# Eight chunks rather than six by seven block products, with the second matrix's sums made in the last part

## The chip, the cores and the metric

The kernel runs on one core of a Trainium2 chip. Its time is the device time of one execution in microseconds. TensorE (PE in the profile) multiplies, VectorE (DVE), ScalarE (ACT) and GpSimd (POOL) do the elementwise work, SyncE (SP) issues the DMAs. "Before" is the kernel as it was, "after" the changed one.

## The reference, cut to what matters

Block-causal attention over 8 batches of 8 heads, 576 tokens, head size 64, and behind it one feed-forward pair of matrices with a leaky ReLU between them, over all 4608 tokens. Everything is fp32.

```python
def _attn_ref(q, k, v):                  # 8, 8, 576, 64
    scores = scale * np.matmul(q, k.transpose(0, 1, 3, 2))
    scores = np.where(block_i >= block_j, scores, -1000000000.0)   # blocks of 64
    scores = scores - np.max(scores, axis=-1, keepdims=True)
    attn = np.exp(scores)
    attn = attn / (np.sum(attn, axis=-1, keepdims=True) + 1e-09)
    return np.matmul(attn, v)

def _moe_ref(x, w_in, w_out):            # 4608 x 512, 512 x 2048, 2048 x 512
    h = x @ w_in
    g = np.maximum(0.01 * h, h)
    return g @ w_out
```

## The kernel before, in words

Every fp32 operand of the feed-forward part is held as two numbers of TensorE's fast format, a high and a low one (`wih`/`wil`, `woh`/`wol`, `xh`/`xl`, `gh`/`gl`), and a product is three matmuls: high by high, high by low, low by high. A pair is made by a cast (ScalarE or VectorE, L300 and L301) and a subtraction (VectorE or GpSimd, L314, L315, L947, L948).

The 4608 tokens are 18 chunks of 256. The first `NP` = 12 go the plain way, 8 units a chunk: `ffn1` (L898) makes two blocks of 128 of the 2048 hidden columns in 24 matmuls of 256 columns, the leaky ReLU (L913) and the split follow, and `ffn2` (L925) adds their part of the output into `p_o` in 12 matmuls of 512 columns. These units lie among the 64 heads of attention: `PACE` says how many heads go by per chunk, `LEAD` how many heads after its last token's head a chunk starts. Heads 0 to 13 use plain fp32 operands; from head 14 on (`PLAIN`) the scores are split products (L573), the probabilities are turned by VectorE and a trip through DRAM (L798, L815, L827), and L713 multiplies them with the values.

The last `2 * TAIL` = 6 chunks are done in pairs, in `tail`. A pair of chunks is a 2 x 2 block product, and Winograd's form makes it with seven block products rather than eight. `first8` makes the first matrix for unit `u` of pair `k` (L1110): seven products of six matmuls of 256 columns, whose results VectorE adds up (L1123) into buffers called `piles`, `more` and a half of `xin`; they are stored to DRAM (`gd`). `second8` (L1239) does the same for the second matrix, 8 steps a pair, four for each half `s`, and each half fills four PSUM banks over its four steps; in its last step `q` = 3 ScalarE copies product 0 out of its bank and VectorE adds the others (L1262). The banks are the list `spots`: half 0 of a pair uses the two banks of the tile `p_s` and the two of `p_v`, half 1 the single-bank tiles `p_h` and `p_o`. `first8` goes round all eight, five a unit. The framework puts in the waits, by what each instruction reads and writes of a tile.

The seven products need sums of blocks of the weights. `sums_ahead` makes them on VectorE while attention runs (L947, into the memory of `xr`), 16 sets, one for each of 8 units of each matrix, and stores them to DRAM (`td`, L986); `PRE0` and `PRE1` say from which head on and how often. In the last part `brought` loads them (L1032) and splits them: `combos` for the first matrix before the last part, `combos2` one block of the second matrix's during it, `combos3` the rest when the first matrix is through with their place. `inputs8` loads a pair's tokens into `x8`, `splits8` makes the seven left operands of them.

The order of the instructions on each engine is written out ahead of time by `Plan`: each step has a rank (for attention the head's number, for a unit the head number at which it is due, in the last part `TR` + 8 `k` + `u`), engines it may run on and an assumed duration, and a list scheduler takes the ready step of the lowest rank. The constants at the head of the file shift these ranks (`RL`, `RP`, `RN`, `RM`, `RG8`, ...). SP's DMAs go out in that order too, and one that waits holds up those behind it. `fourth_stage` gives the memory of attention to the last part.

Of the kernel before, what the change touches and what calls it, by code (L numbers as in the profile page):

```python
# [17 lines left out]
P = 128  # L18
# [6 lines left out]
CH = 256  # L25
# [35 lines left out]
LEAD = 10.984  # L61
LAG = 1.995
RS = -15.318
RG = -8.8
OFF1 = 3.579
SL1 = 23.854
AHEAD = 2.6
# [6 lines left out]
PADD = 4400.167  # L74
HOLD = 266.733
FILL = 235
FILLTO = -148.268
# [9 lines left out]
    [-0.34, -1.77, -1.04, -0.21, -0.2],  # L87
    [-0.63, -6.06, 3.68, 0.48, -3.29],
    [-0.36, -16.86, -0.22, -5.03, 3.79],
    [2.49, -2.84, 0.0, -0.15, -1.95],  # L90
    [1.23, -5.51, -1.24, -1.19, -0.63],
    [-0.02, -6.57, 0.81, -0.09, 1.74],
    [-0.83, 3.75, -0.44, 0.18, -1.57],
    [0.33, 11.3, 1.53, -0.3, 0.55],
    [0.15, 0.48, -1.15, 1.44, -3.96],
# [188 lines left out]
def attention_ffn(ctx: ExitStack, tc: tile.TileContext, q2: bass.AP, k2: bass.AP, qk: bass.AP, v: bass.AP, w_in: bass.AP, w_out: bass.AP, out: bass.AP):  # L284
# [667 lines left out]
    def sums_ahead():  # L952
# [7 lines left out]
        def ahead(j):  # L960
            u, y = j // 2, j % 2
            rank = PRE0 + PRE1 * j
            gate = [("head", min(int(rank), NH - 1))]
            k0, k1, k2, k3 = ([("spare", y, c)] for c in range(4))
            at = lambda c, n=1, y=y: xr.rearrange("p d s -> p (d s)")[:, (4 * y + c) * CH : (4 * y + c + n) * CH]
            if y == 0:
                w0, w1 = wkeys[("wi", u)], wkeys[("wi", u + NU)]
                side = lambda f, low: f32((wil if low else wih)[:, :, f * P : (f + 1) * P])
                four = lambda ap: ap.rearrange("p (d f) -> p d f", f=P)
                sum_of(WIDE, lambda: four(at(1, 2)), lambda: side(u, 0), lambda: side(u, 1), True, rank, w0 + gate, k1 + k2)  # L970
                for h, key in ((0, k0), (1, k3)):
                    part = lambda low, h=h: side(u + NU, low)[:, 2 * h : 2 * h + 2]
                    sum_of(CH, lambda h=h: four(at(3 * h)), lambda part=part: part(0), lambda part=part: part(1), True, rank, w1 + gate, key)
# [401 lines left out]
```

## Time and profile before

| | us |
|---|---|
| timed runs | 1055.57 (median), 1051.42, 1056.27 |
| profiled execution | 1052.72 |
| its span, first to last instruction | 1050.9 |
| PE busy | 1021.6 (97%) |
| PE weight loads busy | 906.6 (86%) |
| VectorE busy | 792.4 (75%) |
| ScalarE busy | 609.8 (58%) |
| GpSimd busy | 353.1 (34%) |

The profile is of one execution. Times are in us, single durations at times in ns. An engine's busy time is the union of its instructions; matmuls follow one another before the one ahead has left the array, so the rows' durations overlap, and the distance from start to start is what one costs. "Idle before" names what ended an engine's wait. The stretches used below: attention with plain fp32 heads until 158 us, with split heads until 732 us, the rest of the plain chunks until 793.5 us, the first matrix of the last part until 925 us, the second until the end.

### The profile page before, as it was taken

The numbers are of one execution on the slowest core, as the hardware profiler recorded it, in microseconds if no ns is written. First come the engines' busy times: TensorE is split into PE (matmuls) and PEld (weight loads), VectorE is DVE, ScalarE is ACT, GpSimd is POOL, SyncE is SP. The second block draws the span as 40 slices with busy tenths as digits, with TensorE's granted clock in tenths as the row PEclk, the third lists the DMA queues.
The fourth block names the chain that finished last, engine by engine and source line by source line (L and its number), as shares of the span: only waits on it lengthen the run. The fifth ranks groups of instructions, "written<-read, shape, count | busy, mean of one in ns | idle before, by whom it ended". The sixth has DMA issues, their size and how long they took to land.

```text
span 1050.9 us, 21285 instructions
## 1 busy us (share of the span) xinstructions
PE 1021.6 (97%) x7336; PEld 906.6 (86%) x7336; DVE 792.4 (75%) x2000; ACT 609.8 (58%) x1435; POOL 353.1 (34%) x347
## 2 busy tenths in 40 slices
PE   7979999999999999999999999999999999989998
PEld 5658889888988888888888888888898999989997
DVE  6888978688978888988898887787065546588774
ACT  7788868476656656666665567575263434443331
POOL 3344327244334434534244344252101223211000
PEclk9999999999999999999999999999999999999999
DMA  6564534766767677676667767674554456765451
GB/s 206 165 195 143 164 107 134 211 206 187 230 183 249 213 229 214 206 221 211 209 204 221 224 213 238 187 225 145 158 202 131 126 172 178 204 211 167 153 163 65
DMA packets 136859, 196.28 MB, mean 187 GB/s; under 512 B 15408, under 2 KB 107312, under 8 KB 136752
## 3 DMA queue, kind: packets, MB, share of 16 engines
q1 hardware_dynamic: 136752, 194.93, 60.7%
q8 instruction: 58, 0.95, 0.4%
q14 instruction: 49, 0.40, 0.1%
HBM read 112.92 MB, written 81.95 MB: 185 GB/s over the span
## 4 chain that ended last, share of the span: by engine, by line
PE 91%; DMA 4%; DVE 2%; ACT 2%; issue 0%; SPq 0%; DVEq 0%; ACTq 0%
PE p_h L898 26%; PE p_o L925 25%; PE p_v L713 7%; PE p_v L573 4%; PE p_s L573 3%; PE p_h L1239 3%; PE p_s L1239 3%; PE p_o L1239 2%; PE p_v L1110 2%; PE p_s L562 2%; PE p_s L1110 2%; PE p_v L1239 2%; PE p_h L1110 2%; PE p_o L1110 2%; PE p_v L668 2%; PE p_v L757 1%
## 5 line engine op out<-in xcount | busy, mean ns | idle before, releaser
L898 PE MATMUL p_h<-big,wih 128*128 128x256 f32 x1216 | 245.5, 280 | 0.4 <-ACT big L300 0.4
L925 PE MATMUL p_o<-woh,big 128*128 128x512 f32 x768 | 236.5, 394 | 0.0
L898 PEld LDWEIGHTS p_h<-big,wih 128*128 128x128 f32 x1216 | 199.0, 188 | 9.9 <-issue 2.2
L315 POOL TENSOR_TENSOR big<-piles,big 128x512 fp32r<-128x512 f32 x80 | 108.2, 1353 | 233.7 <-ACT big L300 216.9
L798 DVE STREAM_TRANSPOSE turn<-prow 128x128 f32<-128x128 f32 (+3 forms) x400 | 146.3, 398 | 16.7 <-POOL prow L633 6.3
L925 PEld LDWEIGHTS p_o<-woh,big 128*128 128x128 f32 x768 | 133.0, 188 | 21.7 <-issue 2.4
L898 PE MATMUL p_h<-big,wil 128*128 128x256 f32 x448 | 122.2, 278 | 0.0
L925 PE MATMUL p_o<-wol,big 128*128 128x512 f32 x384 | 119.5, 393 | 0.0
L913 ACT ACTIVATE piles<-p_h 128x512 f32<-128x512 f32 x96 | 57.2, 595 | 77.9 <-PE p_h L898 75.1
L603 ACT ACTIVATE prow<-p_s,nmrec 128x448 f32<-128x448 f32 (+4 forms) x150 | 83.0, 559 | 32.5 <-DVE nmrec L594 24.7
L633 POOL TENSOR_SCALAR prow<-prow,nmrec 128x448 f32<-128x448 f32 (+4 forms) x89 | 54.4, 618 | 121.2 <-DVE nmrec L620 103.1
L898 PE MATMUL p_h<-xh,wih 128*128 128x256 f32 x320 | 88.1, 280 | 0.0
L315 POOL TENSOR_TENSOR ks<-qk_in,ks 64x576 fp32r<-64x576 f32 x57 | 81.7, 1433 | 17.9 <-ACT ks L300 11.9
L898 PE MATMUL p_h<-xh,wil 128*128 128x256 f32 x320 | 87.4, 278 | 0.0
L603 ACT ACTIVATE prow<-p_v,nmrec 128x576 f32<-128x576 f32 (+1 forms) x150 | 71.5, 484 | 26.2 <-DVE nmrec L594 22.6
L925 PEld LDWEIGHTS p_o<-wol,big 128*128 128x128 f32 x384 | 72.1, 188 | 15.8
L898 PEld LDWEIGHTS p_h<-big,wil 128*128 128x128 f32 x448 | 84.3, 188 | 0.1
L713 PE MATMUL p_v<-turn,vt 128*64 128x256 f32 (+3 forms) x700 | 76.0, 368 | 0.0
L594 DVE TENSOR_REDUCE nmrec<-p_s 128x1 f32<-128x448 f32 (+4 forms) x150 | 72.1, 515 | 0.7
L713 PEld LDWEIGHTS p_v<-turn,vt 128*64 128x64 f32 x700 | 45.4, 137 | 27.9 <-issue 16.9
L635 ACT ACTIVATE prow<-prow,nmrec 128x192 f32<-128x192 f32 (+4 forms) x112 | 59.3, 550 | 11.3 <-DVE nmrec L620 10.8
L300 ACT CAST ks<-qk_in 64x576 fp32r<-64x576 f32 x63 | 42.3, 672 | 40.5 <-PE p_v L573 28.8
(269 smaller groups left out, 2293.7 us busy)
## 6 DMA issues: line engine op xcount, KB each, us to landing
way<-turn SPq DMA_DIRECT2D x50, 448.0 KB, 3.9
way<-turn SPq DMA_DIRECT2D x100, 168.0 KB, 3.7
turn<-way SPq DMA_DIRECT2D x100, 168.0 KB, 3.3
qk_in<-in_qk SPq DMA_DIRECT2D x50, 288.0 KB, 3.5
turn<-way SPq DMA_DIRECT2D x100, 112.0 KB, 3.4
out<-piles SPq DMA_DIRECT2D x36, 256.0 KB, 2.5
raw<-in_w_in SPq DMA_DIRECT2D x16, 512.0 KB, 4.0
raw<-in_w_out SPq DMA_DIRECT2D x16, 512.0 KB, 3.7
```

Of the source, the lines that this page charges most:

```text
L315: ("POOL", pool2(n), lambda: nc.gpsimd.tensor_sub(dst(), one(), two())),
L573: nc.tensor.matmul(ap, later["qs"][z][:, cols], moving, start=first, stop=last)
L594: [("DVE", dve(kw[t]), lambda t=t, ap=ap, flat=flat: nc.vector.tensor_reduce(nm[z][: qn[t], at_col[t] : at_col[t] + 1], ap[: qn[t]], axis= ...
L603: nc.scalar.activation(o, ap[: qn[t]], AF.Exp, bias=nm[z][: qn[t], at_col[t] : at_col[t] + 1], scale=1.0, accum_out=sums[z][: qn[t], at_co ...
L635: ("ACT", act(kw[t], True) + 108, lambda: nc.scalar.mul(p(), p(), by)),
L713: nc.tensor.matmul(dst, later["vt"][z][:, j], src, start=start, stop=stop)
L798: nc.vector.transpose(dst, src.rearrange("p (s b i) -> p s b i", b=4, i=32))
L898: nc.tensor.matmul(p_h[z][:, i, :], w[:, d, f * P : (f + 1) * P], (xl if x else xh[y])[:, d, :], start=first and k == 0 and (u > 0 or i == ...
L913: add([("ACT", act(512), lambda: nc.scalar.activation(g, p_h[z], AF.Prelu, alpha=0.01))], rank, [("h", z)], ["g"])
L925: nc.tensor.matmul(p_o[m], a[:, i, m * P : (m + 1) * P], w[:, u + NU * i, :], start=u == 0 and k == 0, stop=u == NU - 1 and k == 5,)
L1110: nc.tensor.matmul(bank()[:, :CH], stationary(j, u, w, d), operand(j, x)[:, d], start=j not in (4, 6) and n == 0, stop=n == 5, skip_group_ ...
L1239: nc.tensor.matmul(to(), operand(j, low)[0][:, x * P : (x + 1) * P], moving(j, us[x], w), start=q == 0 and m == 0 and j in opens, stop=q = ...
```

## The change

`TAIL` goes from 3 to 4: ten chunks go the plain way, and eight, in four pairs, by seven block products. The second matrix's block sums are no longer among the sets made under attention: `ahead` makes 8 sets, not 16, of the first matrix alone, and `combos2` makes those of the second in the first-matrix phase of the last part, at the units that `SUMS` lists (two in each pair), in the memory of `x8`, on VectorE or GpSimd as the scheduler picks (`op2`); it splits one block at once and stores the other three to DRAM, from which `combos3` loads them as before. In the last part four PSUM tiles of one bank each (`p_x`) take the place of `p_s` and `p_v`, which are given back in `fourth_stage`. The constants of the order have new values, and so have eight numbers of the table `FIRST` (shifts of the first ten heads), which are not shown. The first matrix's sums in `ahead` are the same lines with less indentation.

```diff
-RL = -2.305
-RP = 2.849
-RB = -0.783
-RT = 1.737
+RL = -2.097
+RP = 1.15
+RB = -4.837
+RT = 0.934
 RV = 1.064
-RX = -0.49
-RN = 1.414
-RF = 4.292
-PACE = [5.0, 5.0, 5.67, 4.14, 5.46, 5.0, 4.52, 5.0, 5.55, 5.39, 5.0, 5.17, 5.0, 5.0, 5.0, 5.0, 6.28, 4.59]
+RX = -1.789
+RN = -12.631
+RF = 4.76
+PACE = [6.0, 6.82, 6.0, 6.18, 6.0, 5.97, 5.97, 6.0]
 TWO = True
-TAIL = 3
+TAIL = 4
 TURNS = 4
 TR = 1000.0
-RG8 = -1.0
-RS8 = -3.0
-SUM0 = 2
-RC8 = -8.0
-PRE0 = 22.0
-PRE1 = 2.136
+RG8 = -0.854
+RS8 = -1.748
+SUMS = [1, 2, 9, 10, 17, 18, 25, 26]
+RC8 = -9.359
+PRE0 = 25.352
+PRE1 = 3.071
 PREBY = "DVE"
-RL8 = -6.0
-RT8 = -0.956
-RM = 11.181
-
-LEAD = 10.984
-LAG = 1.995
-RS = -15.318
-RG = -8.8
-OFF1 = 3.579
-SL1 = 23.854
-AHEAD = 2.6
+RL8 = -5.167
+RT8 = -1.106
+RM = -38.787
+
+LEAD = 10.295
+LAG = 2.586
+RS = -15.233
+RG = -9.514
+OFF1 = 2.228
+SL1 = 23.787
+AHEAD = 2.346
...
-PADD = 4400.167
+PADD = 3332.902
...
-FILLTO = -148.268
+FILLTO = -146.792
...
-    p_s = fixed([P, 2, 512], F32, "p_s", pool=psum)
-    p_v = fixed([P, 2, 512], F32, "p_v", pool=psum)
+    p_o = fixed([P, DM], F32, "p_o", 2, pool=psum)
+    pairs = ExitStack()
+    pool = pairs.enter_context(tc.tile_pool(name="pairs", bufs=1, space=PSUM, side="right"))
+    p_s = fixed([P, 2, 512], F32, "p_s", pool=pool)
+    p_v = fixed([P, 2, 512], F32, "p_v", pool=pool)
     p_t = [p_v[:, x] for x in range(2)]
-    p_o = fixed([P, DM], F32, "p_o", 2, pool=psum)
     wide = ExitStack()
     p_w = fixed([P, 2, 512], F32, "p_w", pool=wide.enter_context(tc.tile_pool(name="wide", bufs=1, space=PSUM, reuse_waits="tile")))
     p_h = []
...
     def fourth_stage():
-        for stack in (late, early, tied):
+        for stack in (late, early, tied, pairs):
             stack.close()
+        pool = ctx.enter_context(tc.tile_pool(name="single", bufs=1, space=PSUM, side="right", reuse_waits="tile"))
+        later["single"] = fixed([P, 512], F32, "p_x", 4, pool)
         pool = ctx.enter_context(tc.tile_pool(name="tail", bufs=1, reuse_waits="tile"))
         later["new"] = fixed([P, 3, ND, CH], F32R, "new", None, pool)
         later["x8"] = fixed([P, ND, WIDE], F32, "x8", None, pool)
...
         def sum_of(*args):
             op2(*args, by=PREBY)
-        def ahead(j):
-            u, y = j // 2, j % 2
-            rank = PRE0 + PRE1 * j
+        def ahead(u):
+            rank, y = PRE0 + PRE1 * u, u % 2
             gate = [("head", min(int(rank), NH - 1))]
...
-            else:
-                for x, f in enumerate((u, u + NU)):
-                    w = wkeys[("wo", f)]
-                    sum_of(WIDE, lambda x=x: at(2 * x, 2), lambda f=f: f32(woh[:, f]), lambda f=f: f32(wol[:, f]), True, rank, w + gate, k2 + k3 if x else k0 + k1)
-                sum_of(CH, lambda: at(0), lambda: at(1), lambda: at(0), False, rank, k1, k0)
-                sum_of(CH, lambda: at(1), lambda: at(3), lambda: at(1), False, rank, k3, k1)
-                sum_of(CH, lambda: at(3), lambda: at(3), lambda: at(0), False, rank, k0, k3)
-                sum_of(CH, lambda: at(2), lambda: at(3), lambda: at(2), False, rank, k3, k2)
-            add([("SP", ISSUE, lambda: nc.sync.dma_start(td[u][:, y], at(0, 4)))], rank, k0 + k1 + k2 + k3, [("td", u, y)], lag="pre")
-
-        for j in range(2 * NU):
-            ahead(j)
...
+            add([("SP", ISSUE, lambda: nc.sync.dma_start(td[u][:, 0], at(0, 4)))], rank, k0 + k1 + k2 + k3, [("td", u, 0)], lag="pre")
+
+        for u in range(NU):
+            ahead(u)
     def tail():
         flat = lambda ap: ap.rearrange("p a b -> p (a b)")
-        spots = [(("s", y), lambda y=y: p_s[:, y]) for y in range(2)] + [(("t", y), lambda y=y: p_v[:, y]) for y in range(2)]
+        spots = [(("one", y), lambda y=y: later["single"][y]) for y in range(4)]
         spots += [(("h", y), lambda y=y: flat(p_h[y])) for y in range(2)] + [(("o", y), lambda y=y: p_o[y]) for y in range(2)]
         cells = range(0, CH, BLK)
         xins = [("xin", e) for e in cells]
...
+        old += [(key, y) for key in ("s", "t") for y in range(2)] + [("one", y) for y in range(4)]
...
         def combos2(u, rank):
-            w0 = wkeys[("wo", u)]
-            brought(u, 1, rank, 1, lambda: woh[:, u, CH:], lambda: wol[:, u, CH:], [x for x in w0 if not x[1]], [x for x in w0 if x[1]])
+            w0, w1 = wkeys[("wo", u)], wkeys[("wo", u + NU)]
+            base = 4 * (u % 2)
+            at = lambda y, n=1: flat8()[:, (base + y) * CH : (base + y + n) * CH]
+            d8 = 2 * (u % 2)
+            c0, c1, c2, c3 = (in8(d8 + d, d8 + d + 1, h * CH, (h + 1) * CH) for d in range(2) for h in range(2))
+            for y, (f, w) in enumerate(((u, w0), (u + NU, w1))):
+                op2(WIDE, lambda y=y: at(2 * y, 2), lambda f=f: f32(woh[:, f]), lambda f=f: f32(wol[:, f]), True, rank, w, (c2 + c3) if y else (c0 + c1))
+            op2(CH, lambda: at(0), lambda: at(1), lambda: at(0), False, rank, c1, c0)
+            op2(CH, lambda: at(1), lambda: at(3), lambda: at(1), False, rank, c3, c1)
+            op2(CH, lambda: at(3), lambda: at(3), lambda: at(0), False, rank, c0, c3)
+            op2(CH, lambda: at(2), lambda: at(3), lambda: at(2), False, rank, c3, c2)
+            split(
+                CH, lambda: woh[:, u, CH:], lambda: wol[:, u, CH:], lambda: at(0), rank, c0,
+                [x for x in w0 if not x[1]], [x for x in w0 if x[1]],
+            )
+            add([("SP", ISSUE, lambda: nc.sync.dma_start(td[u][:, 1, CH:], at(1, 3)))], rank, c1 + c2 + c3, [("td", u, 1)], lag="in3")
         def combos3(u, rank):
             brought(u, 1, rank, 0, lambda: sum8(u, 0), lambda: sum8(u, 1), [("S", u, 0)], [("S", u, 1)])
...
                 splits8(k, TR + 8 * k - 2)
             for u in range(NU):
                 first8(k, u, TR + 8 * k + u)
-                y = 8 * k + u - SUM0
-                if y >= 0 and y % 2 == 0 and y // 2 < NU:
-                    combos2(y // 2, TR + 8 * k + u)
+                for y in range(NU):
+                    if int(SUMS[y]) == 8 * k + u:
+                        combos2(y, TR + SUMS[y])
                 if k == TAIL - 1:
                     combos3(u, TR + 8 * TAIL + u // 2 + RT8)
         for n in range(8 * TAIL):
```

## Rows read from the trace of the kernel before

**Rows 1.** Stretches of the span: us, busy us (instructions) of PE, PEld, DVE, ACT, POOL, clock, DMA
```profile
0.00:158.00 158.00, 142.98 (x954) 111.78 (x955) 130.75 (x320) 119.99 (x300) 59.47 (x68) 1.00 0.53 163
158.00:732.00 574.00, 573.90 (x3945) 501.88 (x3944) 474.48 (x1323) 365.71 (x914) 239.56 (x232) 1.00 0.68 207
732.00:793.50 61.50, 61.50 (x414) 53.76 (x413) 25.62 (x47) 26.89 (x55) 8.92 (x8) 1.00 0.53 171
793.50:925.00 131.50, 127.18 (x1064) 125.10 (x1062) 73.09 (x159) 56.06 (x122) 31.39 (x33) 1.00 0.59 171
925.00:1050.90 125.90, 116.09 (x969) 114.06 (x967) 88.42 (x153) 41.19 (x48) 13.80 (x8) 1.00 0.47 147
```

**Rows 2.** Two windows of 25 us, same columns: one under attention, one of the last part
```profile
425.00:450.00 25.00, 25.00 (x169) 21.57 (x168) 22.71 (x64) 16.46 (x43) 11.12 (x12) 1.00 0.69 202
...
950.00:975.00 25.00, 25.00 (x215) 25.00 (x214) 19.23 (x32) 9.25 (x11) 3.45 (x3) 1.00 0.57 175
```

**Rows 3.** Chain of waits in order of time, plain chunks: start us, us, what
```profile
149.11 2.83 PE p_h L898 x24
...
745.22 2.75 PE p_h L898 x24
747.97 4.12 PE p_o L925 x18
```

**Rows 4.** The same chain in the last part, second matrix
```profile
939.09 2.72 PE p_s L1239 x24
...
1000.58 2.83 PE p_h L1239 x24
1003.40 2.12 PE p_o L1239 x18
```

**Rows 5.** Waits of PE after 793 us: waiting, waited for, us in total, times, longest
```profile
PE p_v L1110 <- ACT more L300: 2.0, 1, 2.0
PE p_v L1239 <- DVE piles L1262: 1.5, 3, 0.5
...
PE p_o L1110 <- ACT more L300: 1.0, 1, 1.0
...
PE p_s L1239 <- ACT piles L300: 0.9, 2, 0.5
...
PE p_v L1110 <- DVE piles L1123: 0.4, 2, 0.2
```

**Rows 6.** Timeline near 981 us: start us, us, engine, line, operation, tiles [idle before]
```profile
980.53 0.87 PE L1239 MATMUL p_s<-sum,big 128*128 128x256 f32 x6
...
981.43 0.37 ACT L300 COPY piles<-p_s 128x256 f32<-128x256 f32 x1 [1.47 <-PE p_s L1239]
...
981.86 0.39 PE L1239 MATMUL p_s<-woh,big 128*128 128x256 f32 x1 [0.46 <-ACT piles L300]
```

**Rows 7.** Groups of VectorE, 158 to 732 us: count | busy us, mean ns | idle before
```profile
L947 DVE TENSOR_TENSOR xr<-xr 128x256 f32<-128x256 f32 x64 | 28.5, 445 | 0.2
L634 DVE TENSOR_SCALAR prow<-prow,nmrec 128x192 f32<-128x192 f32 (+4 forms) x66 | 27.5, 445 | 0.6
...
L321 DVE TENSOR_REDUCE p_v<-p_v 64x64 f32<-64x128 f32 x49 | 14.2, 289 | 25.8 <-PE p_v L573 25.5
L947 DVE TENSOR_TENSOR xr<-woh,wol 128x512 f32<-128x512 f32 x16 | 11.8, 748 | 0.0
```

**Rows 8.** Exponents and first block products (ns min/median/max, first to last start); a split's timeline
```profile
L603 ACT ACTIVATE prow<-p_v,nmrec x150: 293/411/756, 158.2 to 732.0; 128x576 f32<-128x576 f32 x50, 128x192 f32<-128x192 f32 x50, 64x64 f32<-64x64 f32 x50
...
764.78 0.62 ACT L300 CAST new<-x 128x512 fp32r<-128x512 f32 x1
...
L1110 PE MATMUL p_s<-new,wih x48: 276/281/281, 793.7 to 911.0; 128*128 128x256 f32 x48
```

**Rows 9.** Timeline near 787 us, VectorE and GpSimd
```profile
786.98 1.30 POOL L315 TENSOR_TENSOR big<-piles,big 128x512 fp32r<-128x512 f32 x1 [20.67 <-ACT big L300]
...
787.24 1.31 DVE L947 TENSOR_TENSOR wol<-wol,woh 128x256 fp32r<-128x256 f32 x1 [3.48 <-ACT woh L300]
```

More of the change, by code (lines that the diff above doesn't have):

```diff
@@ L86 @@
 FIRST = [
-    [-0.34, -1.77, -1.04, -0.21, -0.2],
+    [-1.37, -1.77, -1.04, -0.11, 7.51],
     [-0.63, -6.06, 3.68, 0.48, -3.29],
-    [-0.36, -16.86, -0.22, -5.03, 3.79],
+    [-1.46, -16.86, -0.22, -5.03, 3.79],
     [2.49, -2.84, 0.0, -0.15, -1.95],
-    [1.23, -5.51, -1.24, -1.19, -0.63],
+    [1.23, -5.51, -1.24, -1.19, 3.67],
     [-0.02, -6.57, 0.81, -0.09, 1.74],
     [-0.83, 3.75, -0.44, 0.18, -1.57],
-    [0.33, 11.3, 1.53, -0.3, 0.55],
-    [0.15, 0.48, -1.15, 1.44, -3.96],
+    [-1.45, 11.3, 1.44, -0.3, 0.55],
+    [0.15, 0.69, -1.34, 2.68, -3.96],
     [1.34, -0.81, -0.2, -0.65, -0.94],
@@ L958, in sum_of @@
             op2(*args, by=PREBY)
-        def ahead(j):
-            u, y = j // 2, j % 2
-            rank = PRE0 + PRE1 * j
+        def ahead(u):
+            rank, y = PRE0 + PRE1 * u, u % 2
             gate = [("head", min(int(rank), NH - 1))]
             k0, k1, k2, k3 = ([("spare", y, c)] for c in range(4))
[L965 to L973, printed above, removed]
-                sum_of(CH, lambda: at(3), lambda: at(0), lambda: at(3), True, rank, k0, k3)
-                sum_of(CH, lambda: at(0), lambda: at(1), lambda: at(0), False, rank, k1, k0)
-                sum_of(CH, lambda: at(1), lambda: at(3), lambda: at(1), False, rank, k3, k1)
-                sum_of(CH, lambda: at(2), lambda: at(2), lambda: at(1), False, rank, k1, k2)
-            else:
-                for x, f in enumerate((u, u + NU)):
-                    w = wkeys[("wo", f)]
-                    sum_of(WIDE, lambda x=x: at(2 * x, 2), lambda f=f: f32(woh[:, f]), lambda f=f: f32(wol[:, f]), True, rank, w + gate, k2 + k3 if x else k0 + k1)
-                sum_of(CH, lambda: at(0), lambda: at(1), lambda: at(0), False, rank, k1, k0)
-                sum_of(CH, lambda: at(1), lambda: at(3), lambda: at(1), False, rank, k3, k1)
-                sum_of(CH, lambda: at(3), lambda: at(3), lambda: at(0), False, rank, k0, k3)
-                sum_of(CH, lambda: at(2), lambda: at(3), lambda: at(2), False, rank, k3, k2)
-            add([("SP", ISSUE, lambda: nc.sync.dma_start(td[u][:, y], at(0, 4)))], rank, k0 + k1 + k2 + k3, [("td", u, y)], lag="pre")
@@ L988, in sums_ahead @@
-        for j in range(2 * NU):
-            ahead(j)
+            at = lambda c, n=1: xr.rearrange("p d s -> p (d s)")[:, (4 * y + c) * CH : (4 * y + c + n) * CH]
+            w0, w1 = wkeys[("wi", u)], wkeys[("wi", u + NU)]
+            side = lambda f, low: f32((wil if low else wih)[:, :, f * P : (f + 1) * P])
+            four = lambda ap: ap.rearrange("p (d f) -> p d f", f=P)
+            sum_of(WIDE, lambda: four(at(1, 2)), lambda: side(u, 0), lambda: side(u, 1), True, rank, w0 + gate, k1 + k2)
@@ new lines, in ahead @@
+            for h, key in ((0, k0), (1, k3)):
+                part = lambda low, h=h: side(u + NU, low)[:, 2 * h : 2 * h + 2]
+                sum_of(CH, lambda h=h: four(at(3 * h)), lambda part=part: part(0), lambda part=part: part(1), True, rank, w1 + gate, key)
+            sum_of(CH, lambda: at(3), lambda: at(0), lambda: at(3), True, rank, k0, k3)
+            sum_of(CH, lambda: at(0), lambda: at(1), lambda: at(0), False, rank, k1, k0)
+            sum_of(CH, lambda: at(1), lambda: at(3), lambda: at(1), False, rank, k3, k1)
@@ L991, in tail @@
+            sum_of(CH, lambda: at(2), lambda: at(2), lambda: at(1), False, rank, k1, k2)
+            add([("SP", ISSUE, lambda: nc.sync.dma_start(td[u][:, 0], at(0, 4)))], rank, k0 + k1 + k2 + k3, [("td", u, 0)], lag="pre")
+        for u in range(NU):
+            ahead(u)
     def tail():
         flat = lambda ap: ap.rearrange("p a b -> p (a b)")
-        spots = [(("s", y), lambda y=y: p_s[:, y]) for y in range(2)] + [(("t", y), lambda y=y: p_v[:, y]) for y in range(2)]
+        spots = [(("one", y), lambda y=y: later["single"][y]) for y in range(4)]
```

## The prediction

> **What bounds the kernel now.** I read the busy times by stage first. Look at the PE column: 573.90 of 574 us between 158 and 732 us, 61.50 of 61.5 in the stretch behind it, then 127.18 of 131.5 and 116.09 of 125.9 in the two halves of the last part [rows 1]. So TensorE is the bound from 158 us on; before that it is idle for 15.0 us, and in the last part for 14.1 us together. No stretch has a granted clock other than 1.00, the 2.4 GHz level, so the clock is no term here. VectorE is the second engine, 474.48 of 574 us, 82.7% [rows 1]. Then I read the chain of waits in order of time for the price of a unit of work [rows 3, 4], the waits of PE in the last part for what its idle time is [rows 5], the timeline at one of them [rows 6], and VectorE's groups between 158 and 732 us for what the change takes from it [rows 7]. Of the 1052.72 us of the profiled execution the span is 1050.9; 1.8 us lie around it and stay.
>
> **The change, part by part.**
>
> *Two chunks leave the plain product.* One chunk is 8 units, each of 24 matmuls of 256 columns and 12 of 512. The 24 take 2.75 to 2.83 us, twelve of the wide ones 4.12 x 12/18 = 2.75 us [rows 3]. A unit is 5.50 to 5.58 us, middle 5.54, and sixteen units are 88.0 to 89.3 us. I take 88.7. All of it is on the path, since PE has no idle time there.
>
> *One more pair by seven products.* A pair is 8 x 7 products of six 256-column matmuls for the first matrix and as many for the second: 112 products, 672 matmuls. Four products take 2.72 to 2.83 us [rows 4], so 112 take 76.2 to 79.2 us. A full window of the last part has 215 matmuls in 25 us [rows 2], 116.3 ns each, and gives 78.1. I take that. These two terms alone are -10.6 us; bounds -8.8 to -13.1.
>
> *A tile for each bank.* In the last part PE waits 1.5 us in 3 waits of p_v for a VectorE sum and 0.9 in 2 of p_s for a ScalarE copy while it makes the second matrix [rows 5]. The timeline shows that these are waits for another bank of the same tile: the product j = 3 goes to the second bank of p_s, and starts at 981.86 exactly when ScalarE's copy of product 0 out of the first bank, begun at 981.43, is over [rows 6]. In the second half of each pair, where the sums lie in p_h and p_o, already one tile a bank, the chain runs from 1000.58 through p_h into p_o without a gap [rows 4]. So the wait comes from the tile and should go. Its price: six matmuls from 980.53 at 0.118 would end at 981.24, the next starts at 981.86, a loss of 0.62 against 0.46 shown as idle; so 2.4 us in five waits become 2.4 + 5 x 0.16 = 3.2. In the first matrix two waits of p_v for VectorE, 0.4 in all [rows 5], I take for the same sort, 0.7 with that addition. Together -3.9 us. Bounds: 0, if the sum that was waited for is needed a moment later by the same product anyway, and -5, if waits too short for the view go along. What is late next there is only a bank that is truly in use; eight banks at five a unit leave three products, 2.1 us, of slack.
>
> *What the fourth pair brings of its own.* The waits of the first matrix for ScalarE to fill a buffer whose store is still landing are 2.0 + 1.0 us over three pairs [rows 5]: +1.0 us for a fourth. Bounds 0 to 2.2, the longest alone with its restart. The gaps where the second matrix begins come once, as now.
>
> *Second-matrix sums into the last part.* Of the 16 sets that VectorE makes under attention eight go: 8 x (2 x 0.748 + 4 x 0.445) = 26.2 us [rows 7], and eight stores of the results on SP's queue. That time hides under PE now, so it gives nothing at once; it pays for the squeeze below. In the last part the same 3.28 us come in eight units, two a pair, each with a 256-column split (0.445, as the row of that shape) that replaces the one made now after a load, and a store on SP's queue; eight small loads on that queue go. A unit of the last part is 7 x 0.70 = 4.9 us of PE; VectorE has five sums of 256 columns in it, and with the added set and its split 6 x 0.445 + 3.28 = 5.95. So it falls 1.05 us behind in each of two units, less than the 2.1 us of slack in the banks, and has room in the next four. Behind the set's store on SP's queue stand the next results' stores and the load of the next pair's input, which now shares its buffer with the sums; four units, 20 us, lie between them and its use. I take +1.0; bounds 0 and 8 x 1.05 = 8.4, if no slack is carried.
>
> What the trace shows of VectorE beside GpSimd: a 256-column subtraction took 1.31 us, where such an operation takes 0.445 on average [rows 7], when GpSimd's of 1.30 had started 0.26 before it [rows 9]. The Trainium skill (SBUF — State Buffer, section "SBUF: two separate sides") says why: a VectorE operation with two SBUF inputs and a GpSimd operation share one port pair as an exclusive lock, and the later one waits for all of the other. The trace agrees at this place. By that rule the 48 moved operations can each be stretched, where GpSimd is busy 31.39 of 131.5 us [rows 1]; it is the rule that speaks against moving them, and its outcome is the second rival.
>
> *The new order before the last part.* Attention must now fit into less time. The first 14 heads end at 158 us; the last exponent of the other 50 starts at 732.0, the first block product at 793.7 [rows 8]. Of the 61.5 us between them the last head's values, the store and reload of its output and the first split take until 764.78 [rows 8]; I estimate that 40 would do. The last part should begin at 793.7 - 88.7 = 705, so the exponents must end at 665: 50 heads in 507 us rather than 574. VectorE's work in that time is 474.5 - 26.2 = 448.3 us (the two chunks' own part in it left in), 88.4% of 507. One window shows 22.71 of 25 us, 90.8%, with PE at 25.00 [rows 2], and part of VectorE's idle time now is waiting for PE itself, 25.5 us in one group [rows 7], so I hold it possible. Normalising, 27.5 us on VectorE [rows 7], may also go to ScalarE or GpSimd, busy 365.71 and 239.56 of 574 [rows 1]. Bounds 0 and the first rival's 35 us; I take +2. The first 158 us get other ranks too; nothing here prices them, so 0, bounds -5 (a third of the 15.0 us of idle time) and +3.
>
> The sum: -88.7 + 78.1 - 3.9 + 1.0 + 1.0 + 2.0 = -10.5 us. From the profiled execution that is 1042.2; it lies 2.85 us below the median of the timed runs, 1055.57, one of which (1051.42) is faster still. From the median it would be 1045.1. I say 1043.
>
> **The rivals.**
>
> *VectorE sets the pace of attention (slower).* Place: 158 to 665 us. If VectorE can be kept no busier than the 82.7% it shows now, 448.3 us of work take 542, PE has run out of plain chunks by then, and the last part starts 35 us late: 1043 + 33 = 1076. The kernel is as slow as before from a loss of 12.5 us, that is at 86.3% of VectorE, and slower by 0.5% at 85.4%. For it: the shares that the whole stretch has now. Against it: PE is full there, so 82.7% is what PE lets VectorE do, not what it can do. Chance 0.12.
>
> *The last part turns from PE to VectorE (no change).* The sums cost their bound of 8.4 rather than 1.0, the waits for a bank come back as waits for VectorE (3.9 lost): 1043 + 7.4 + 3.9 = 1054. For it: the stretched operation in [rows 9]; against it: VectorE is busy 73.09 of 131.5 us there, 88.42 of 125.9 behind it [rows 1]. Chance 0.11.
>
> *The split tile does not do what it says.* The waits stay where they were: 1043 + 3.9 = 1047, still faster. Against it is p_h beside p_s [rows 4, 6]. Chance 0.12.
>
> *More is gained.* Units at their dear end (89.3), products at their cheap end (76.2), terms of +4 gone, 5 us of the early idle time gone: 1043 - 0.6 - 1.9 - 4 - 5 = 1031 or so. Chance 0.15. My forecast, 1037 to 1050 around 1043, has 0.50.
>
> **How the numbers follow.** About 0.5%, 5 us, is what a measurement of this kernel can tell from no change; the four times shown differ by 4.85. Faster: 0.50 + 0.12 + 0.15, less a little for the edge of the forecast's own range, 0.76. Same: 0.12. Slower: 0.12. The range goes from the best case, 1031, past the second rival to a first rival of one third its size, 1057; the rest of the first rival, and little else, is left out.
>
> **What would show it.** Right: 1920 rather than 2304 matmuls of 256 columns in L898's groups and 2688 rather than 2016 in the two block-product lines; the first block product near 705 us; no PE wait for ScalarE's or VectorE's copies in the middle of a second-matrix product; VectorE near 88% in the attention stretch with PE still full. Wrong: PE idle between 158 us and the last part, ended by VectorE or by a turned tile's DMA (first rival); PE waits in the units with the added sums (second); the waits of [rows 6] on the new tile. If the first block product comes later than 717 us the forecast is lost.

## The result and the profile after

| | before | after |
|---|---|---|
| timed runs beside each other, median | 1052.86 (1051.42 to 1056.27) | 1039.72 (1038.56 to 1044.41) |
| ratio of the two, 95% interval | | 0.9883 [0.9852, 0.9914] |
| profiled execution, its span | 1052.72, 1050.9 | 1044.29, 1042.4 |
| the same kernel once more, 5 runs | 1055.56 | 1042.27 (1040.57 to 1044.3), 0.9878 [0.9862, 0.9895] |

The change makes the kernel 1.2% faster, 12 to 13 us; 1043 had been forecast. The second set of runs of the unchanged kernel after has a profile of its own (1042.27, span 1040.4), called "again" below. The spans differ by only 8.5 and 10.5 us, because the profiled execution of before is among its faster ones: three later sets of its runs have medians between 1054.92 and 1056.27.

Stretches of after, as [rows 1]: until the first split scores, until the last ones, the plain chunks left over, first matrix, second matrix.

```profile
0.00:160.80 160.80, 144.32 (x939) 111.79 (x940) 128.24 (x307) 117.84 (x296) 60.01 (x72) 0.97 0.51 158
160.80:664.00 503.20, 502.63 (x3477) 437.45 (x3476) 407.54 (x1188) 358.93 (x922) 271.81 (x252) 1.00 0.74 224
664.00:711.50 47.50, 47.50 (x321) 40.80 (x320) 21.31 (x45) 22.07 (x46) 12.43 (x11) 1.00 0.66 212
711.50:874.00 162.50, 157.23 (x1355) 155.23 (x1354) 112.99 (x231) 74.32 (x166) 66.39 (x68) 1.00 0.62 186
874.00:1042.40 168.40, 161.38 (x1349) 160.36 (x1347) 122.60 (x212) 55.32 (x66) 26.35 (x17) 0.99 0.50 156
```

PE is still full from the first split scores to the last part, in a stretch that is 88 us shorter. VectorE, the third busy column, fills 407.54 of 503.20, 81%; in before it was 82.7% [rows 1]. The squeeze has not raised its share. The last part is longer by a pair and leaves PE 12.3 us idle in four pairs, where three left 14.1.

The marks between the stages are first and last starts in views by line: the split scores of before, then the split scores and the first block products of after and of again (columns as in [rows 8]).

```profile
L573 PE MATMUL p_v<-ks,qs x350: 218/293/402, 154.6 to 727.9; 128*128 128x288 f32 x100, 128*128 128x192 f32 x50, 128*128 128x128 f32 x25
```
```profile
L577 PE MATMUL p_v<-ks,qs x350: 218/293/352, 160.8 to 663.1; 128*128 128x288 f32 x100, 128*128 128x192 f32 x50, 128*128 128x128 f32 x25
...
L1119 PE MATMUL p_x<-new,wih x128: 276/276/281, 711.6 to 866.6; 128*128 128x256 f32 x128
```
```profile
L577 PE MATMUL p_v<-ks,qs x350: 218/293/402, 157.3 to 660.7; 128*128 128x288 f32 x100, 128*128 128x192 f32 x50, 128*128 128x128 f32 x25
...
L1119 PE MATMUL p_x<-new,wih x128: 276/276/281, 709.3 to 864.6; 128*128 128x256 f32 x128
```

With the first block product of before at 793.7 [rows 8] the span splits in three. "Early" ends with the first split scores, "front" with the first block product.

| us | early | front | last part | span |
|---|---|---|---|---|
| before | 154.6 | 639.1 | 257.2 | 1050.9 |
| after | 160.8 (+6.2) | 550.8 (-88.3) | 330.8 (+73.6) | 1042.4 (-8.5) |
| again | 157.3 (+2.7) | 552.0 (-87.1) | 331.1 (+73.9) | 1040.4 (-10.5) |
| forecast | 0 | -86.7 | +76.2 | -10.5 |

Of the 3.5 us between the two early stages much may be the clock, since the kernel is the same: in the window from 50 to 75 us, after's mean granted clock was 0.83, part of it at the 1.2 GHz level, and again's 1.00.

The counts came as forecast: the page has 1024 + 384 + 256 + 256 = 1920 matmuls of 256 columns at L902 (L898 before), and 2688 in the two block-product lines. PE's waits from 700 us on, as [rows 5]:

```profile
PE p_x L1119 <- ACT piles L300: 2.5, 2, 1.7
PE p_x L1248 <- ACT big L300: 1.7, 2, 1.2
PE p_o L1119 <- DVE piles L1132: 1.6, 1, 1.6
PE p_x L1248 <- DVE big L951: 1.0, 2, 0.5
...
PE p_h L1119 <- ACT more L300: 0.4, 1, 0.4
```

None is for a reader of another bank in the second matrix. What is left at L1248 comes where that matrix begins, for its first operands (`big`). At the place that answers to [rows 6] ScalarE's copy of product 0 begins 0.20 us after PE has begun to fill another bank. These are rows of PE and ScalarE, in order of time:

```profile
975.11 0.87 PE L1248 MATMUL p_x<-sum,big 128*128 128x256 f32 x6
975.81 0.28 PE L1248 MATMUL p_x<-woh,big 128*128 128x256 f32 x1
```
```profile
975.31 0.37 ACT L300 COPY piles<-p_x 128x256 f32<-128x256 f32 x1 [0.77 <-PE p_x L1248]
```

In [rows 6] the copy came 0.90 us after that start, when the product into the tile's other bank was through, and PE then waited for the copy; the next product started 1.33 us after the one ahead of it. Here it starts after 0.70. The shared tile made each engine wait for the other.

### The profile page after: what moved, and what is told of

Its sections match the earlier page's. It is cut to its first block, busy times and chain, and to the rows that moved or that the text cites. A ratio compares the mean times of both kernels' runs of the same rounds, so it can differ in the third digit from the quotient of the medians.

```text
span 1042.4 us, 21854 instructions
## 1 busy us (share of the span) xinstructions
PE 1013.1 (97%) x7432; PEld 905.6 (87%) x7432; DVE 792.7 (76%) x1980; ACT 628.5 (60%) x1495; POOL 437.0 (42%) x419
## 4 chain that ended last, share of the span: by engine, by line
PE 84%; DMA 7%; ACT 3%; DVE 2%; issue 1%; SPq 1%; POOL 1%; DVEq 0%; ACTq 0%; POOLq 0%
PE p_o L929 20%; PE p_h L902 20%; PE p_v L717 7%; PE p_x L1248 7%; PE p_h L1248 4%; PE p_x L1119 4%; PE p_v L577 4%; PE p_s L577 4%; PE p_o L1248 3%; PE p_s L566 2%; PE p_h L1119 2%; PE p_o L1119 2%; DMA gd<-more 2%; PE p_v L672 2%; DMA gd<-piles 2%
## 5 line engine op out<-in xcount | busy, mean ns | idle before, releaser
L902 PE MATMUL p_h<-big,wih 128*128 128x256 f32 x1024 | 204.4, 280 | 0.4 <-ACT big L300 0.4
L929 PE MATMUL p_o<-woh,big 128*128 128x512 f32 x640 | 191.5, 394 | 0.3 <-ACT piles L300 0.3
L902 PEld LDWEIGHTS p_h<-big,wih 128*128 128x128 f32 x1024 | 165.7, 188 | 5.7 <-issue 1.0
L315 POOL TENSOR_TENSOR ks<-qk_in,ks 64x576 fp32r<-64x576 f32 x83 | 122.9, 1480 | 54.9 <-DVE p_v L591 28.0
L929 PEld LDWEIGHTS p_o<-woh,big 128*128 128x128 f32 x640 | 113.5, 188 | 20.6 <-issue 1.3
L315 POOL TENSOR_TENSOR big<-piles,big 128x512 fp32r<-128x512 f32 x64 | 84.8, 1325 | 102.8 <-ACT big L300 81.3
L902 PE MATMUL p_h<-big,wil 128*128 128x256 f32 x384 | 104.9, 278 | 0.0
L929 PE MATMUL p_o<-wol,big 128*128 128x512 f32 x320 | 99.7, 393 | 0.0
L637 POOL TENSOR_SCALAR prow<-prow,nmrec 128x192 f32<-128x192 f32 (+4 forms) x94 | 61.1, 656 | 73.9 <-DVE nmrec L624 39.8
L639 ACT ACTIVATE prow<-prow,nmrec 128x320 f32<-128x320 f32 (+4 forms) x154 | 81.7, 566 | 3.5 <-DVE nmrec L624 3.3
L902 PEld LDWEIGHTS p_h<-big,wil 128*128 128x128 f32 x384 | 72.3, 188 | 0.2
L717 PEld LDWEIGHTS p_v<-turn,vt 128*64 128x64 f32 x700 | 46.5, 137 | 28.5 <-issue 16.3
L902 PE MATMUL p_h<-xh,wih 128*128 128x256 f32 x256 | 69.8, 278 | 0.0
L902 PE MATMUL p_h<-xh,wil 128*128 128x256 f32 x256 | 69.8, 278 | 0.0
L300 ACT CAST big<-piles 128x512 fp32r<-128x512 f32 x74 | 45.8, 619 | 18.3 <-PE p_o L929 17.4
```

Of the source, the lines that this page charges most:

```text
L315: ("POOL", pool2(n), lambda: nc.gpsimd.tensor_sub(dst(), one(), two())),
L637: ("POOL", pool1(kw[t]), lambda: nc.gpsimd.tensor_scalar(p(), p(), by, 1.0, op0=ALU.mult, op1=ALU.mult)),
L639: ("ACT", act(kw[t], True) + 108, lambda: nc.scalar.mul(p(), p(), by)),
L717: nc.tensor.matmul(dst, later["vt"][z][:, j], src, start=start, stop=stop)
L902: nc.tensor.matmul(p_h[z][:, i, :], w[:, d, f * P : (f + 1) * P], (xl if x else xh[y])[:, d, :], start=first and k == 0 and (u > 0 or i == ...
L929: nc.tensor.matmul(p_o[m], a[:, i, m * P : (m + 1) * P], w[:, u + NU * i, :], start=u == 0 and k == 0, stop=u == NU - 1 and k == 5,)
```

## The experiments

Ten runs were timed beside before, one of them after once more. Theory 1, that of the forecast: the gain is what a pair saves on TensorE (88.7 against 78.1) and a few us of waits that the tiles bring; sums and squeeze cost next to nothing. Rivals: the sums cost VectorE time that PE waits for; or the new order makes the gain.

**The tiles alone.** Before, with the four single-bank tiles in the last part and nothing else; the order of instructions is before's on every engine.

```diff
...
-        for stack in (late, early, tied):
+        for stack in (late, early, tied, pairs):
...
+        later["single"] = fixed([P, 512], F32, "p_x", 4, pool)
...
-        spots = [(("s", y), lambda y=y: p_s[:, y]) for y in range(2)] + [(("t", y), lambda y=y: p_v[:, y]) for y in range(2)]
+        spots = [(("one", y), lambda y=y: later["single"][y]) for y in range(4)]
```

> The kernel before with one part of the change: four single-bank tiles in the last part in place of the two two-bank tiles; the order of the instructions on every engine is the same. My theory (a wait comes from the shared tile): 3.9 us less than before, bounds 3 to 5, and no PE wait inside the second-matrix products for another bank's reader. Rival (the reader is needed a moment later anyway, or the gain is all from the fourth pair and the order): no difference, within 1.5 us of before.

1047.82 against 1056.27, ratio 0.9915 [0.9896, 0.9935]: 7 to 11 us, not 3.9. By the stages (155.9, 638.3, 249.9) all of it is in the last part, 7.3 us less, and most of that is in the *first* matrix. From start to start its 1008 matmuls took 123.3 us before and 117.0 now, the second matrix 126.1 and 125.1. The timeline shows what I had not seen. First before, one stretch on PE and on ScalarE, then this kernel on both:

```profile
809.22 0.96 PE L1110 MATMUL p_v<-new,sum 128*128 128x256 f32 x6 [1.98 <-ACT more L300]
```
```profile
808.79 0.37 ACT L300 COPY more<-p_v 128x256 f32<-128x256 f32 x1 [1.93 <-DMA gd<-more]
```
```profile
807.18 0.84 PE L1115 MATMUL p_x<-new,sum 128*128 128x256 f32 x6
807.86 0.28 PE L1115 MATMUL p_h<-new,wih 128*128 128x256 f32 x1
...
809.66 0.39 PE L1115 MATMUL p_x<-big,wih 128*128 128x256 f32 x1 [0.28 <-ACT more L300]
```
```profile
809.23 0.37 ACT L300 COPY more<-p_x 128x256 f32<-128x256 f32 x1 [2.13 <-DMA gd<-more]
```

ScalarE waits 2 us in both for a store out of `more` before it can copy a bank. With the shared tile PE's next product, into the *other* bank of `p_v`, waits with it (1.98). With single tiles PE goes on through `p_x` and `p_h` and loses 0.28 us three products later. So the 2.0 us that [rows 5] put down to a full buffer were the tile's too. Where the second matrix begins PE's waits for its operands grew, from 3.0 us in before to 4.2 here, 2.6 + 1.2 of them for `big`; that is why only 1.0 us is left of what the tiles give there.

Waiting is not all of the 6.3 us in the first matrix. PE's waits there fell from 4.3 to 1.2 us. Where matmuls follow one another without a wait, they stood 115.8 ns apart on average in before and 113.8 here, which is 2 us over the 1008. The medians of one group tell it too: 281 ns in before [rows 8], 276 here.

```profile
L1115 PE MATMUL p_x<-new,wih x96: 276/276/281, 794.2 to 909.2; 128*128 128x256 f32 x96
```

Whether the tiles brought the closer distance is not shown (see the last section).

**The tiles taken out of after.** The same edit backwards.

> The changed kernel with the two two-bank tiles kept in the last part; same order on every engine. My theory: four pairs at 0.62 + 0.68 us each and some waits in the first matrix bring 5 to 7 us back, so 1045 to 1047. Rival: the tile does nothing here, 1040 as the changed kernel.

1046.96, as expected, ratio 0.9919 [0.99, 0.9938]; after has 0.9878 [0.9862, 0.9895], so the tiles are worth 4.3 us ± 2.7 in the new order. The waits of [rows 5] are back; PE's waits from 705 us on:

```profile
PE p_v L1243 <- DVE piles L1266: 1.5, 3, 0.5
PE p_s L1243 <- ACT piles L300: 1.4, 3, 0.5
```

So the two parts overlap. The tiles give 8.5 us (medians) to the old order and about 4 to the new one. In the new order the first matrix has no long wait for `more` even with the old tiles: PE waits 3.8 us there in four pairs, and 5.2 in after. What the tiles give to it lies in the second matrix, where PE's waits go from 6.6 us to 2.7.

**The sums under attention, as before.** After, with the 16 sets of before (PRE1 halved so that they end at about the same head).

```diff
-PRE1 = 3.071
+PRE1 = 1.536
...
-        for u in range(NU):
-            ahead(u)
+        for j in range(2 * NU):
+            ahead(j)
...
```

> The changed kernel with the second matrix's eight sets of sums made under attention again, sixteen sets at half the distance. VectorE gets 26.2 us more between 160 and 664 us, 463.7 rather than 437.5 of 503 us, 92%. Theory A (VectorE has room up to the 91% of single windows, PE sets the pace): about as the changed kernel, 1038 to 1042. Theory B (at 87% VectorE is already the limit, and moving the sums is what makes room for the fourth pair): the exponents end up to 30 us later, PE runs dry before the last part, 1050 to 1068.

1128.87, ratio 1.069 [1.067, 1.0709], 7% slower, far above both theories. Their 437.5 us are misread: that is the column of the weight loads in after. VectorE had 407.54 us, so 16 sets make some 434 us, 86% of 503 and not 92%. Stretches of its span:

```profile
400.00:540.00 140.00, 76.15 (x386) 58.28 (x385) 114.48 (x347) 76.92 (x210) 65.79 (x70) 0.71 0.76 238
540.00:672.10 132.10, 132.10 (x924) 115.11 (x923) 106.09 (x293) 89.42 (x235) 65.47 (x61) 1.00 0.73 215
672.10:798.10 126.00, 126.00 (x833) 112.17 (x833) 36.36 (x75) 41.27 (x77) 26.81 (x23) 1.00 0.30 95
```

PE is busy for 76.15 of the 140 us between 400 and 540 us, at a mean granted clock of 0.71, and has 126 us of plain work left afterwards that should have lain among attention's. VectorE is at 82% even there. The timeline tells why: the high half of a chunk's split at 353.80, the low half of it, on VectorE, at 535.61.

```profile
353.80 1.05 ACT L300 CAST big<-xin 128x1024 fp32r<-128x1024 f32 x1 [1.83 <-DMA xin<-xt]
```
```profile
535.61 1.22 DVE L314 TENSOR_TENSOR big<-xin,big 128x1024 fp32r<-128x1024 f32 x1
```

No plain unit of that chunk can start before the 1.2 us operation at 535.61. The constant `RS` ranks these splits by some 15 heads behind attention's work and the sums; with 26 us more of ranked work on VectorE the planner found no free place for 180 us. This became a theory of its own: the loss is not VectorE's time but one short operation of low rank.

**That theory's test.** The same kernel, and the split ranked ahead.

```diff
-RS = -15.233
+RS = 12.0
```

> Sixteen sets under attention as in the run sums_ahead, but the chunk split (RS) gets a rank 27 heads earlier, so that it goes ahead of attention's work on VectorE. In sums_ahead PE had no plain unit from 408 to 537 us: ScalarE had cast the chunk's high half at 353.8, VectorE made its low half at 535.6. Theory A (the split of the lowest rank is what starves when VectorE always has other work): PE stays full under attention and the time is within 10 us of the changed kernel, 1040 to 1050. Theory B (VectorE's sum of work is the limit at 91%): the exponents end up to 25 us later than at 664 and the time stays above 1060.

1050.18 (1037.7 to 1054.55), ratio 0.9915 [0.9882, 0.9949]: by the ratios some 82 of the 86 us are gone by one constant.

```profile
160.50:674.60 514.10, 511.60 (x3536) 444.91 (x3534) 428.48 (x1217) 363.96 (x931) 282.70 (x265) 1.00 0.76 229
```

VectorE works 428.48 us here, 21 more than in after, and PE stays full. What the sums under attention cost when nothing starves is 0 to 8 us; the runs spread too far to say more, and what this value of `RS` does to after itself was not tried.

**The sums left out of the last part.** The split and the store take what lies in the buffer.

```diff
...
-            for y, (f, w) in enumerate(((u, w0), (u + NU, w1))):
-                op2(WIDE, lambda y=y: at(2 * y, 2), ...
-            op2(CH, lambda: at(0), lambda: at(1), lambda: at(0), False, rank, c1, c0)
...
```

> The changed kernel with the six sums a set left out of the last part (the split and the store use what lies in the buffer), so the price of making the second matrix's sums there. My prediction's term: 1.0 us, bounds 0 and 8.4. Theory (they hide beside PE): 0 to 2 us less than the changed kernel. Rival (VectorE and GpSimd fall behind in these units and the waits for stored buffers come from that): 4 to 8 us less.

1044.84 (1042.52 to 1047.64), ratio 0.9903 [0.9884, 0.9923]: not faster than with them. Groups of after between 711.5 and 874 us, first VectorE, then GpSimd:

```profile
L951 DVE TENSOR_TENSOR x<-woh,wol 128x512 f32<-128x512 f32 x6 | 4.1, 680 | 0.0
```
```profile
L952 POOL TENSOR_TENSOR x<-woh,wol 128x512 f32<-128x512 f32 x9 | 13.0, 1442 | 5.1 <-DVE new L951 5.1
```

GpSimd makes most of the wide sums, at twice the time each. In their own stage they are not free. Without them the first matrix took 157.0 us from start to start, against 159.7 in after and 160.2 in again, and PE's waits in it came to 2.2 us against 5.3 and 4.8. The 3 us are lost where the second matrix begins, in one wait of PE (of this kind after has 1.7 us there, again 2.4):

```profile
PE p_x L1242 <- ACT big L300: 6.3, 1, 6.3
```

The mean granted clock of the 25 us from 875 us on is 0.86 behind that wait, 0.93 in after. The planner also makes another order once the sums are out, so the 3 us are not theirs alone.

**Three pairs in the new order.** To price the pair: TAIL 3, one PACE of 5.08, eight places for the sums in three pairs; then the same with the split ranked ahead.

```diff
-PACE = [6.0, 6.82, 6.0, 6.18, 6.0, 5.97, 5.97, 6.0]
+PACE = [5.08]
...
-TAIL = 4
+TAIL = 3
...
-SUMS = [1, 2, 9, 10, 17, 18, 25, 26]
+SUMS = [1, 2, 3, 9, 10, 11, 17, 18]
```

> The changed kernel with three pairs rather than four: twelve chunks the plain way at 5.08 heads each; single-bank tiles, sums in the last part and the other constants as changed. Theory (the fourth pair is worth the 10.6 us of matmuls less 1 us of waits): 1049 to 1051, that is 3 to 4 us under before, which the tiles give. Rival (the gain is in the new order and the tiles, the pair only moves work): 1040 to 1043.

> Three pairs, twelve chunks as in the run six, with the same early rank for the chunk split. six lost 25 us to the same starving at 450 to 500 us and so did not price the pair. Theory A (by stages: against the kernel before with single-bank tiles the pair takes 82.6 us out of the front and adds 80.9 at the end): 2 to 4 us above the changed kernel, about 0.991 of before. Theory B (my prediction: 10.6 less 2): 8 to 9 us above the changed kernel, about 0.997 of before.

1076.78, ratio 1.0201 [1.0183, 1.022], and with RS 1061.14, 1.0054 [1.0037, 1.0072]; both lie above all that was expected. Neither prices the pair: both leave far too much plain work behind attention (first three columns: stretch, length, PE).

```profile
667.70:817.00 149.30, 149.30 (x983) 133.37 (x982) 37.03 (x75) 47.86 (x89) 30.37 (x24) 1.00 0.26 81
```
```profile
670.00:800.30 130.30, 130.30 (x863) 116.16 (x863) 34.68 (x71) 43.32 (x82) 27.27 (x23) 1.00 0.29 91
```

In before that stretch was 61.5 us [rows 1]. The early rank of the split takes back 15.6 us of the loss; the rest I put down to an order fitted to ten plain chunks that has twelve to place. Better is the tiles-alone kernel against again, whose order constants were each fitted to their number of pairs; that prices the pair, the moved sums and the new order together.

**After again.** Nothing changed.

> The changed kernel once more, for a second profile and a time on the same chip as the runs beside it. In the profile at hand the second matrix's matmuls stand 118 ns apart throughout and the first matrix's 113; the five times fell in two groups, 1039 and 1044. If the distance is drawn anew in every execution, the second matrix can show 113 here and the time then be some 5 us lower; if it belongs to the instructions, it is 118 again and the groups come from elsewhere. Ratio to before 0.985 to 0.991.

Its time and profile stand in the section on the result; the second matrix ran at 118 ns again. Tiles alone to again: early +1.4, front -86.3, last part +81.2, sum -3.7 by the profiles; 0.9915 to 0.9878 by the ratios, 3.9 us ± 2.7.

**The old order for the new kernel.**

> The kernel after with the constants of the order of the kernel before; PACE alone is set to 6.09 heads a chunk, so that the ten plain chunks go by in the same 64 heads less the lead. Eight chunks by block products, the sums of the second matrix in the last part and a tile for each bank stay. Theory A, the new order is what makes room for the fourth pair under attention: with the old one the plain units come late, PE runs dry under attention and makes up for it behind it, the first block product comes 30 us or more after 711.6, and the time is 1070 to 1095. Rival, the pair and the tiles bring the gain by themselves and the order is a trimming of a few us: 1042 to 1050.

1089.9 (1089.45 to 1091.92), ratio 1.0334 [1.0312, 1.0356], so the time is theory A's; the mechanism is the reverse of what I wrote. PE hardly runs dry under attention (548.55 of 553.20 us); it runs dry behind the last scores:

```profile
156.30:709.50 553.20, 548.55 (x3758) 478.83 (x3756) 452.60 (x1273) 358.67 (x903) 238.78 (x225) 1.00 0.69 207
709.50:742.90 33.40, 11.69 (x58) 6.81 (x56) 7.84 (x27) 5.78 (x17) 0.75 (x1) 0.65 0.55 167
742.90:1088.20 345.30, 325.76 (x2688) 322.09 (x2688) 243.49 (x457) 136.36 (x238) 90.55 (x79) 0.97 0.55 171
```

The plain units go out too soon and attention ends at 709.5 rather than 664, with no plain unit left. The last heads' turn through DRAM, which plain work covers in after (47.5 us with PE full), lies bare (58 matmuls in 33 us, mean granted clock 0.65), and the last part is 14.5 us longer. These constants were fitted to another kernel, so the time measures that misfit; it does not show that no other order would do. On the timeline of PE:

```profile
728.91 1.94 PE L717 MATMUL p_v<-turn,vt 128*64 128x512 f32 x2 [9.99 <-DMA turn<-way]
...
742.93 0.58 PE L1119 MATMUL p_x<-new,wih 128*128 128x256 f32 x1 [6.79 <-ACT new L300]
```

**Ten chunks.** Five pairs, eight plain chunks, an order fitted to them more briefly, with small shifts of other constants that are not shown.

```diff
...
-PACE = [6.0, 6.82, 6.0, 6.18, 6.0, 5.97, 5.97, 6.0]
+PACE = [8.92]
...
-TAIL = 4
+TAIL = 5
...
-RS = -15.233
+RS = 13.526
...
```

> Ten chunks in five pairs by block products, eight the plain way, with an order fitted to that for some minutes (rank of the chunk split 13.5, one PACE of 8.92, other small shifts), rest as after. Theory A, TensorE alone sets the time, and a fifth pair brings what the fourth did by its nominal terms: 81 us more in the last part, 87 to 89 less before it, 1033 to 1037. Rival, the other engines set the pace of attention once the plain chunks are this few: the last part of 412 us would have to begin near 625, the last exponents near 580, 420 us after the first split scores. VectorE's 407 us of work there would fill 97% of that; at the 91% of its fullest window it takes 448, so PE has gaps under attention and the last part begins at 650 or later: 1062 to 1085, PE busy under 90% between 160 us and the last exponents.

1089.86 (1085.59 to 1093.42), ratio 1.0316 [1.0284, 1.0349]: the rival's side, a little beyond its range.

```profile
156.80:649.80 493.00, 455.66 (x3057) 391.72 (x3056) 403.44 (x1181) 334.40 (x883) 273.72 (x264) 0.95 0.76 227
...
679.30:1091.60 412.30, 398.35 (x3360) 395.57 (x3360) 286.69 (x540) 175.04 (x303) 113.28 (x102) 0.99 0.57 175
```

The last part is 412.3 us, as expected: 249.9, 331.1 and 412.3 for three, four and five pairs, 81.2 us for each. The front is 522.5, only 29.5 shorter than again's where 87 were to be had. Of the missing 57, 37 us are idle PE under attention; the mean granted clock of 0.95 in that stretch, part of it at the 1.2 GHz level behind such waits, can account for about 20 more (an estimate: 5% of 493 us is 25). My reason for it does not hold as put: VectorE is at 82% of that stretch, not at 91%. PE waits for ScalarE's exponents there, 15.6 us in one group:

```profile
PE p_v L717 <- ACT prow L607: 15.6, 6, 5.9
```

I read this as too little plain work left to stand between a head's dependent steps; no run tests it apart. How much of the loss a longer fitted order would win back is open.

## Why the prediction was right, step by step

*Two chunks leave (-88.7) and the squeeze (+2.0).* Together -86.7; the front shows -88.3 and -87.1. Right. The first block product came at 711.6 and 709.3, inside the 717 named, late mostly by what the early part lost.

*First rival, VectorE sets the pace.* It did not come, and neither did the sign "VectorE near 88%": it is 81%. The premise, that 448.3 us of work stay on VectorE, was wrong: 407.5 are left. The forecast took only normalising to be movable. Groups under attention, VectorE and GpSimd of before (keys), then VectorE and GpSimd of after:

```profile
L314 DVE TENSOR_TENSOR ks<-qk_in,ks 64x576 fp32r<-64x576 f32 x41 | 33.1, 808 | 1.3 <-ACT ks L300 0.2
```
```profile
L315 POOL TENSOR_TENSOR ks<-qk_in,ks 64x576 fp32r<-64x576 f32 x57 | 81.7, 1433 | 17.9 <-ACT ks L300 11.9 <-DMA turn<-way 2.3
```
```profile
L951 DVE TENSOR_TENSOR xr<-xr 128x256 f32<-128x256 f32 x32 | 13.7, 427 | 0.2
L314 DVE TENSOR_TENSOR ks<-qk_in,ks 64x576 fp32r<-64x576 f32 x15 | 12.7, 849 | 0.5 <-ACT ks L300 0.3
L638 DVE TENSOR_SCALAR prow<-prow,nmrec 128x448 f32<-128x448 f32 (+3 forms) x26 | 12.0, 461 | 0.6
```
```profile
L315 POOL TENSOR_TENSOR ks<-qk_in,ks 64x576 fp32r<-64x576 f32 x83 | 122.9, 1480 | 54.9 <-DVE p_v L591 28.0 <-ACT ks L300 18.5 <-PE p_h L902 3.5
```

The 26.2 us of sums went as worked out (28.5 to 13.7 in the 256-column group [rows 7], and the whole wide group of 11.8). Beyond it, 40 normalising operations left VectorE (66 to 26, 15.5 us [rows 7]). So did 26 subtractions of keys (41 to 15), which GpSimd took at 1.48 us each (57 to 83). GpSimd went from 239.56 to 271.81 us, and PE stayed full. What the fourth pair did need was an order fitted to it: with the old one the kernel is 3.3% slower than before and the front is 586.6 us, 36 longer than after's, with VectorE at 452.6 of 553.2 us. The forecast had the risk (bound 35 us) in the right place, but named the wrong cause.

*One more pair (+78.1).* The last part of again is 81.2 us longer than with the tiles alone; the forecast's comparable terms, 78.1 + 1.0 + 1.0, make 80.1. Right. Two nominal terms alone gave -10.6; with the costs around them the pair, the moved sums and the order gave about -3.7 beside single tiles and -8.6 ± 2 beside the old ones, where the forecast's terms without the tile make -6.6. How much of that is the pair and how much the order no run tells apart.

*A tile for each bank (-3.9).* The mechanism was right. In the order before, for which the term was worked out, its size was too small: 7.3 us by the profile, 8.5 by the medians. The step that failed is the reading of the 2.0 us of "p_v L1110 <- ACT more L300" in [rows 5] as a genuine wait for a store, booked in the +1.0 for the fourth pair. It was ScalarE that had to wait; PE waited only because the tile was shared. The lower bound of -5 left it out too. Some 2 us of the surplus are the closer distance of the matmuls, which nothing in the forecast names. In the new order, in which after runs, the tiles are worth 4.3 ± 2.7 us, the size forecast.

*Sums in the last part (+1.0), and the second rival.* Leaving them out won nothing (2.6 us slower by the medians, ± 2.7 by the ratios), so the rival's 7.4 us did not come. The term's place was not quite right: the first matrix is some 3 us longer with the sums, and the wait where the second begins takes that up. PE waits for VectorE's sums of products there 1.6 us in after, once. The Trainium skill ("SBUF — State Buffer", section "SBUF: two separate sides"), which has VectorE and GpSimd shut each other out of a shared port, agreed with [rows 9] at one operation, 1.31 us where 0.445 is usual. No run shows what such stretches cost in the last part by themselves.

*The first 158 us (0).* They cost 2.7 us in again, 1.3 of which the tiles-alone kernel shows too, and 6.2 in after's profile with its lower clock. The bound of +3 held but for that.

*The clock (no term).* That was read from the profile of before, which stands at 1.00 throughout. Every other profiled execution has a fall to the 1.2 GHz level behind the waits where the second matrix begins (the last section). In after some sixteen matmuls stand 213 ns apart there rather than 118, about 1.5 us that the forecast has nowhere.

The parts overlap, so how the total came right depends on the order in which they are counted. From before over the tiles alone two errors meet: the tiles gave 3 to 5 us more than forecast, and pair, sums and order 3 us less. From before over the old tiles in the new order both terms lie within the noise of the forecast's. That 1043 lies within 1 to 3 us of the two medians is closer than its parts are known, and so in part luck. "The split tile does nothing" is refuted by both tile experiments, "more is gained" by the time.

## What to carry to other kernels

When PE waits for a copy out of a bank that it does not itself need, look at what the copying engine waits for: a tile of two banks hands that wait on, even one for a DMA, and one tile for each bank ends it without a change of order. When a list scheduler ranks work by due time, one short operation of low rank that gates a long chain can starve behind work that is merely ranked higher; before you call the engine full, look for an operand whose high half is made long before its low half. An experiment that undoes one part of a fitted kernel measures the misfit as well, so price a part between two kernels that were both fitted or, as with the tiles, with the order held equal.

## What the runs showed of the hardware that was not expected

The 256-column block products stand at one of two distances with the granted clock at 1.00: 24 of them took 2.72 us (113 ns each) in after's first matrix and 2.83 us (118 ns) in its second, and they keep to one distance for hundreds of matmuls. The chain of waits of after, in order of time:

```profile
728.17 2.72 PE p_x L1119 x24
...
914.50 2.83 PE p_h L1248 x24
919.44 19.79 PE p_x L1248 x168
```

The distance changes at some waits, and also where PE waited for nothing, as in after at 875.7 us. The second matrix ran at 117.4 to 117.8 on average in all but one execution, the first between 113.5 and 115.8; over 2688 matmuls the two differ by some 12 us, as much as this change is worth. What sets it is open. Whether it explains why single runs of after lie near 1039 or near 1044 is open too: no run near 1039 was profiled, and the two that were (1044.29 and 1042.27) both ran the second matrix at 118.

After a short gap at the start of the second matrix (waits of 1.21 and 0.52 us from 879.4 on) the clock fell: twelve matmuls from 882.25 took 2.64 us, and the window shows a mean granted clock of 0.93, some of it at the 1.2 GHz level. The same window has 0.93 in again and in after with the old tiles, and the tiles-alone kernel has 0.93 from 920 to 945 us, each behind waits for `big` at this place; before, with waits of 1.0 us and less there, has 1.00 from 915 to 940 us.

```profile
875.00:900.00 25.00, 22.21 (x169) 21.40 (x169) 18.10 (x29) 9.67 (x12) 5.78 (x4) 0.93 0.66 201
```
